# FFT convolution, last tile: four u and v buffers, sums on GpSimd, output jobs moved into the tile before, other transfers and fewer filler products

## The chip, the core and the metric

The kernel runs on one NeuronCore of a Trainium2 chip. The core has five engines that run side by side, each with its own queue in program order: TensorE (PE, matrix products; its weight loads are listed as PEld), VectorE (DVE), ScalarE (ACT), GpSimd (POOL) and SyncE (SP). SP and ACT also issue DMA transfers; sixteen DMA engines carry them. Operands lie in SBUF (128 partitions), products go into PSUM, which has eight banks. Engines wait for each other through semaphores.

The metric is device time in microseconds (us). Before the change it is 263.94 us, the median of three runs (263.47 to 264.06).

## The reference

The reference computes a circular 7 x 7 convolution of an image with 96 channels to 96 channels by a two-dimensional FFT of 224 x 224 points:

```python
H = W = 224; C = 96; K = 7
x: (1, H, W, C) bf16        w: (K, K, C, C) bf16
wp = jnp.pad(w, ((0, H - K), (0, W - K), (0, 0), (0, 0)))
Xf = rfft2(x.astype(float32), axes=(1, 2))
Wf = rfft2(wp.astype(float32), axes=(0, 1))
Yf = einsum('bhwi,hwio->bhwo', Xf, Wf)
y  = irfft2(Yf, s=(H, W), axes=(1, 2)).astype(bfloat16)
```

## The kernel before

The kernel doesn't transform the whole image. Along the height it cuts the 224 rows into eight strips of 28 rows and uses a short transform of each strip (17 frequencies, `NS`; the first and the last are real, `REAL`). Along the width it convolves directly, with taps saved by a fast algorithm that needs sums and differences of neighbouring pixel planes. The width is cut into seven tiles of 32 pixels, tile 0 to tile 6; `TL` is 6, the last. Everything below is about tiles 5 and 6.

Each tile passes through three stages, and the stages of neighbouring tiles run at the same time.

- *Forward transform* (`a_jobs`): products of the input pixels in `xn` with the transform matrix; the results are cast into `xf`. The jobs of tile t + 1 run during tile t, so during tile 6 there are none, and the two `xn` buffers lie idle.
- *Rounds* (`b_round`, line 595), one for each of the 17 frequencies. A round multiplies `xf` and the planes `J` with the transformed weights `WF` into two PSUM banks. The half rounds are counted 0 to 33; after the first bank's products and at the end of the round, `fills` inserts jobs of other stages. ACT scales a part of the first bank into `tt_`; DVE computes u from the first bank and `tt_`, and v from `tt_` and the second bank; the sum of v and u goes into `yf`. The tiles `tt_`, u and v come from `tv_pool` (line 830), two buffers each, so u and v of a round wait for the sum two rounds earlier. The sum (`ysum`, line 671) runs on POOL, or on DVE where `ydve` is set: before, in rounds that also make planes, and in the last tile also in rounds 14, 15 and 16 (line 968). The real rounds 0 and 16 have one DVE sum from a copy by ACT and a bank.
- *Planes* (`jit`, line 563): three DVE operations that make the planes `J` for the next group of three rounds. They are issued in rounds 0, 3, 6, 9 and 12, behind v. A POOL sum of the same round is ordered behind the planes by a semaphore.
- *Put*: after each group of three rounds `yf` is written to a scratch tensor in DRAM, by SP, and in the last tile by ACT in the round that follows, behind that round's scaling (`puts`, line 659). The put after round 16 goes on SP.
- *Output jobs* (`c_jobs`, line 748), eleven for each tile: `load_t` (line 704) reads the scratch tensor back into a tile `tt` with the frequencies in the partitions; a job is two products with the inverse matrix `Gm`, two casts (ACT or DVE, by a planned balance) and, after every second job or so, a DMA to the output. `CQ` (line 43) says how many old and new jobs run during a tile: in tile 5 five of tile 3 and eight of tile 4; in tile 6 three of tile 4 and five of tile 5. `k0` and `k1` are the half rounds between which `pace` spreads them. Only four `tt` tiles and one wide tile `tt2` exist, so a load is issued when an older tile's jobs are done (`pump`, line 802).

The last tile has its own end. Its scratch tensor is split by frequency (`SLAST`): rounds 0 to 8 in `scra` (three puts), then 9 to 11, 12 to 14 and 15 to 16 in three `scrb` (the fourth, fifth and sixth put). The first reloads bring `scra` back in round 11, two transfers. `load_b` (line 723) brings back the three `scrb` parts: the second, third and fourth reload. After round 16 come the six remaining output jobs of tile 5, the first eight products with `GA` on the reloaded `scra` (`first`), filler products on a zero tile `wu` that add nothing to the banks (`WARM`, line 994), and the second products with `GB` (`second`), which need all of `scrb`. Each result is cast into an output tile and written out in eight transfers.

The order on each engine is that in which the program issues the instructions. PSUM banks are handed out in turn, eight in all: two for each round and two for each output job, so a round's bank is the one used four rounds ago, or two rounds ago where every round has a job.

Since helpers record all operations, the profile shows line 99 for nearly all of them; groups are told apart by their tiles: `pb` is a PSUM bank, `yo` or `J` an output tile (the third `J` buffer serves as one).

Of the kernel before, what the change touches and what calls it, by code (L numbers as in the profile page):

```python
# [39 lines left out]
YBUF = 4  # L40
JGB = ((0, 3), (3, 6), (6, 9), (9, 12), (12, 15), (15, 17))
LAG = 4
CQ = {2: (11, 0), 3: (11, 3), 4: (8, 6), 5: (5, 8), 6: (3, 5)}
SH0 = (0, 6, 13, 17)
SH2 = (0, 8, 13, 17)
SH3 = (0, 8, 17)
MERGE = ()
NP2 = 0
WARM = 26
HEAD = ("w",) * 6 + ("x0", "w", "w", "h0", "h1", "w", "w", "x1", "w", "w")  # L50
W1 = 30
ZC = 48
# [12 lines left out]
def kernel(  # L65
# [95 lines left out]
    RB = [sum(KB[:i]) for i in range(NL - 1)]  # L161
    assert sum(KB) == 128
    XW = 2 * TW * C
    xn_bufs = [cpool.tile([R, XW + 32], BF16, name=f"xn{i}") for i in range(2)]

    wtmp_cm = tc.tile_pool(name="wtmp", bufs=1, side="right")
    wtmp = wtmp_cm.__enter__()
# [395 lines left out]
    def jit(t, g):  # L563
# [25 lines left out]
            sub(Jb[:, 5:7, i0:i1], Jb[:, 0:4:2, i0:i1], Jb[:, 1:4:2, i0:i1], ALU.add, 2 * PP * (c1 - c0)),  # L589
        ]  # L590

    yf_cur = {}
    held_x = None

    def b_round(t, s, mid, end, ydve=False, planes=()):
        xf = xf_tiles[t][0:C]
        Jb = jbuf[(t, s)]
        xv = xf.rearrange("c p r s w j -> c p r s (w j)")
        st = {
            0: (Jb[:, 4], xv[:, 0, 1, s], xv[:, 0, 0, s]),  # L600
            1: (Jb[:, 6], Jb[:, 3], Jb[:, 2]),
            2: (Jb[:, 5], Jb[:, 1], Jb[:, 0]),
        }
        for (y0, y1) in (YGRPL if t == TL else YGRP):
            if s == y0:
                yf_cur[t] = (yf_pool.tile([128, YMAX, 2, 2, C], BF16, name="yf"), y0, y1)
        yf, y0, y1 = yf_cur[t]
        yv = yf[:, s - y0]

        def conv(bank, col, m, part, add=False, both=False):  # L610
            pl = st[m][part] if s not in REAL else (xv[:, 0, :, s], Jb[:, 2:4], Jb[:, 0:2])[m][:, part]
            tp = TAPS[m]
            for k, tp_ in enumerate(tp):
                o, wv = bank[:, col:col + C], WF[0:C, slot(s, part), tp_, :]
                if both:
                    o, wv = bank[:, col:col + 2 * C].rearrange("p (m o) -> p m o", m=2), wv.unsqueeze(1).to_broadcast([C, 2, C])
                TE.matmul(o, lhsT=pl[:, (HALO - k) * NJ:(HALO - k) * NJ + 128], rhs=wv,
                          start=(k == 0 and not add), stop=(k == len(tp) - 1 and not both and m != 2 or not add and not both and k == len(tp) - 1))
        b0, b1 = bank(), bank()
        merge = t < 2 and s in MERGE  # L620
        tt_ = tv_pool.tile([128, 4 * C], F32, name="tt_")
        if s in REAL:
            for part in range(2):
                conv(b0, part * C, 0, part)
            held = SE.copy(out=tt_[:, 0:2 * C], in_=b0[:, 0:2 * C])
            if t == s == 0:
                nonlocal held_x
                held_x = held
            mid()
            for mi, m in enumerate((2, 1)):  # L630
                for part in range(2):
                    conv(b1, (mi * 2 + part) * C, m, part)
            VE.tensor_tensor(out=yv.rearrange("p r m o -> p m r o"),
                             in0=tt_[:, 0:2 * C].rearrange("p (r o) -> p r o", o=C).unsqueeze(1).to_broadcast([128, 2, 2, C]),
                             in1=b1[:, 0:4 * C].rearrange("p (m r o) -> p m r o", m=2, r=2), op=ALU.add)
            load["a"] += 110 + 0.9 * 192
            load["v"] += 540
            for f in planes:
                f()
            end()  # L640
        else:
            v = tv_pool.tile([128, 2, 2, C], F32, name="v")
            if merge:
                conv(b0, 2 * C, 0, 0, both=True)
                conv(b0, 2 * C, 2, 0, add=True)
                conv(b0, 3 * C, 1, 0, add=True)
                conv(b0, 0, 0, 1)
                conv(b0, C, 0, 2)
                SE.mul(out=tt_[:], in_=b0[:, 0:4 * C], mul=-0.5)
                u, pr = tt_[:, 2 * C:4 * C].rearrange("p (m o) -> p m o", m=2), tt_[:, 0:2 * C]  # L650
            else:
                for part in range(3):
                    conv(b0, part * C, 0, part)
                conv(b0, 3 * C, 2, 0)
                conv(b0, 4 * C, 1, 0)
                u = tv_pool.tile([128, 2, C], F32, name="u")
                SE.mul(out=tt_[:, 0:3 * C], in_=b0[:, 0:3 * C], mul=-0.5)
                pr = tt_[:, C:3 * C]
            if puts:
                puts.pop(0)()  # L660
            if not merge:
                VE.scalar_tensor_tensor(out=u[:], in0=b0[:, 3 * C:5 * C].rearrange("p (m o) -> p m o", m=2), scalar=-0.5,
                                        in1=tt_[:, 0:C].unsqueeze(1).to_broadcast([128, 2, C]), op0=ALU.mult, op1=ALU.add)
            mid()
            for mi, m in enumerate((2, 1)):
                for pi, part in enumerate((1, 2)):
                    conv(b1, (mi * 2 + pi) * C, m, part)
            VE.scalar_tensor_tensor(out=v.rearrange("p m r o -> p m (r o)"),
                                    in0=pr.unsqueeze(1).to_broadcast([128, 2, 2 * C]), scalar=-2.0,
                                    in1=b1[:, 0:4 * C].rearrange("p (m q) -> p m q", m=2), op0=ALU.mult, op1=ALU.add)  # L670
            def ysum(eng):
                return eng.tensor_tensor(out=yv.rearrange("p r m o -> p m r o"), in0=v[:],
                                         in1=u.unsqueeze(2).to_broadcast([128, 2, 2, C]), op=ALU.add)
            if ydve:
                ysum(VE)
            last = None
            for f in planes:
                last = f()
            if not ydve:
                y = ysum(GE)  # L680
                if len(planes) > 1:
                    tc.add_manual_dep(y.ins, last.ins.name, SYNC, reason="sum after planes")
            load["a"] += 490 if merge else 410
            load["v"] += (560 if ydve else 250 if t < 2 else 0) + (560 if merge else 900)
            end()
        if s == y1 - 1:
            dst, yo0 = scr_tiles[t], 0
            if t == TL:
                i = sum(s >= v for v in SLAST[1:])
                dst, yo0 = scr_tiles[(t, i)], SLAST[i]  # L690

            def put(eng=DE):
                eng.dma_start(out=dst.rearrange("w j s e -> (w j) s e")[:, y0 - yo0:y1 - yo0],
                              in_=yf[:, 0:y1 - y0].rearrange("p s r m o -> p s (r m o)"))
            if t == TL and s < NS - 1:
                puts.append(lambda: put(SE))
            else:
                put()
# [5 lines left out]
    def load_t(t, gi, h):  # L704
        tt = t2_pool.tile([128, 12, 2 * C], BF16, name="tt2") if gi == 2 else t_pool.tile([128, 8, 2 * C], BF16, name="tt")
        tt_tiles[(t, gi, h)] = tt
        sv = scr_tiles[t].rearrange("w j s (r e) -> (j s r) w e", r=2)
        if gi < 2:
            dma(tt[0:112, 0:8], sv[gi * 3 * FR:gi * 3 * FR + 112, h * 8:(h + 1) * 8])
        else:  # L710
            r0 = 6 * FR
            for p0, p1 in ((0, 64), (64, 2 * FR)):
                dma(tt[p0:p1], sv[r0 + p0:r0 + p1, 0:12])
            for j in range(2):
                dma(tt[2 * FR:3 * FR, 4 * j:4 * j + 4], sv[r0 + j * FR:r0 + (j + 1) * FR, 12:16])

    TW2 = 2 * TW * C
    tl_all = xf_bufs[(TL + 1) % 2].rearrange("c p r s w j -> c (p r s w j)")
# [211 lines left out]
    for t in range(2, NT):  # L930
# [9 lines left out]
            add(4 if t == 2 else 0, 26, a_jobs(t + 1))  # L940
        nold, nnew = CQ[t]
        k1 = 2 * NS if t < TL else 2 * NS - 8
        k0 = {2: 15, TL: 6}.get(t, 3)
        km = k0 + -(-(k1 - k0) * nold // (nold + nnew))
        add(k0, km, cj[:nold])
        cn = c_jobs(t - 1)
# [6 lines left out]
        for s in range(NS):  # L953
            now = ()
            if s in plan:
                g = plan[s]
                now = jit(t, g + 1) if g + 1 < len(JGB) else jit(t + 1, 0)
            if s == 2 and t == 2:
                queue_c(0)
            if s == (3 if t in (2, TL) else 2):  # L960
                queue_c(t - 1)
            if t in (3, 4):
                next(gp, None)
            if t == TL and s == SA + 2:
                sv = scr_tiles[(TL, 0)].rearrange("w j s (r e) -> (j s r) w e", r=2)
                for g in range(2):
                    dma(tl_a[g], sv[g * (2 * KA - KAP):g * (2 * KA - KAP) + KAP])
            b_round(t, s, fills(qs, 2 * s), fills(qs, 2 * s + 1), bool(now) or (t == TL and s >= NS - 3), now)
    tail[0] = 1
    load["v"], load["a"] = 1000.0, 0.0  # L970
    while cj:
        cj.pop(0)()
    assert not pend
    for i in range(NL - 1):
        load_b(i)
    for f in outs:
        f()
# [63 lines left out]
```

## Time and profile before

| | us |
|---|---|
| median of three runs | 263.94 |
| the profiled execution's own time | 263.47 |
| its span | 261.7 |
| PE busy | 252.0 |
| DVE busy | 218.4 |
| ACT busy | 196.7 |
| POOL busy | 97.6 |

The profile page lists busy time by engine, the chain of work that ended last, followed back from the last instruction, and groups of instructions. In the timeline each line has the start, the duration, the engine and the operation with its output and inputs; brackets at the end tell how long the engine idled before it and what ended that. SPq and ACTq are the queues of DMA issues of SP and ACT; their durations are those of the issue. The trace also holds the landings of every transfer, one for each DMA engine that took part.

Times are counted from the start of the span. Tile 5's rounds run from about 186 to 216 us, the last tile's from 216 to 243; the end takes from 243 to 261.7. In this execution round 0 of the last tile starts its first products on `xf` at 216.36, round 3 at 220.30, round 6 at 225.60, round 9 at 231.44, round 12 at 236.85 and round 16 at 242.29.

### The profile page before, as it was taken

To read this page: it belongs to the slowest core of one execution; us is meant where nothing else is said; L and a number is where in the kernel's file an instruction comes from. 1 tells how busy PE (TensorE), PEld (TensorE's weight loads), DVE (VectorE), ACT (ScalarE), POOL (GpSimd) and SP (SyncE) were. 2 spreads that over 40 slices of the span, in tenths; PEclk is the share of its full clock that TensorE was granted. 3 is DMA by queue.
4 is the path that set the end of the run, shared out by engine and by line. 5 is a ranking of instruction groups with operands and counts; after the bars stand their busy time and mean duration, and the time that the engine had idled before them with its cause. 6 is when DMAs were issued, how large, how long until landed. Compare 5 with 4: busy or idle time off the path is not lost.

```text
span 261.7 us, 11987 instructions
## 1 busy us (share of the span) xinstructions
PE 252.0 (96%) x5054; PEld 233.2 (89%) x5054; DVE 218.4 (83%) x462; ACT 196.7 (75%) x470; POOL 97.6 (37%) x152
## 2 busy tenths in 40 slices
PE   8999999999999999999999999999999999989983
PEld 2889999999989999989999998999999999979652
DVE  6799998899999889868887788878989799989724
ACT  8889978697745967988988799887988853555423
POOL 7782224464656633232223322334123423423000
PEclk9999999999999999999999999999999999999999
DMA  7995104611111697997967596878849842886996
GB/s 177 272 186 135 48 6 140 177 48 48 48 51 71 183 255 138 302 286 192 271 188 222 143 278 206 212 200 255 275 139 193 288 140 83 206 232 185 236 249 201
DMA packets 47278, 46.88 MB, mean 179 GB/s; under 512 B 35696, under 2 KB 38452, under 8 KB 47224
## 3 DMA queue, kind: packets, MB, share of 16 engines
q1 hardware_dynamic: 46504, 44.64, 62.6%
q10 hardware_dynamic: 720, 1.47, 1.7%
q8 instruction: 39, 0.64, 1.1%
q14 instruction: 15, 0.12, 0.2%
HBM read 24.76 MB, written 21.33 MB: 176 GB/s over the span
## 4 chain that ended last, share of the span: by engine, by line
PE 74%; DVE 10%; DMA 8%; issue 4%; ACT 1%; POOL 1%; SPq 1%; DVEq 0%; ACTq 0%
PE pb L99 68%; PE ps L99 6%; DVE J L99 5%; DMA xn<-in_x_dram 3%; DVE WF L99 2%; DMA tt<-scr 2%; DMA xf<-scrb 2%; DMA scrb<-yf 1%; DVE v L99 1%; POOL yf L99 1%; DVE yf L99 1%; DMA scr<-yf 1%; DVE u L99 1%; SPq L99 1%; ACT xf L99 0%
## 5 line engine op out<-in xcount | busy, mean ns | idle before, releaser
L99 PE MATMUL pb<-WF,J 96*128 96x96 bf16 x2821 | 162.4, 206 | 2.1 <-DVE u L99 0.8
L99 PEld LDWEIGHTS <-J 96*128 96x128 bf16 x2821 | 138.0, 98 | 11.0 <-issue 3.7
L99 POOL TENSOR_TENSOR yf<-v,u 128x384 bf16<-128x384 f32 x79 | 81.4, 1044 | 139.7 <-issue 86.3
L99 ACT CAST xf<-pb 96x408 bf16<-96x408 f32 (+6 forms) x140 | 65.1, 492 | 3.4 <-PE pb L99 1.4
L99 PE MATMUL pb<-WF,xf 96*128 96x96 bf16 x952 | 59.9, 206 | 0.2
L99 DVE TENSOR_TENSOR J<-xf 96x456 bf16<-96x456 bf16 (+3 forms) x85 | 56.0, 698 | 0.0
L99 PEld LDWEIGHTS <-xf 96*128 96x128 bf16 x952 | 47.1, 98 | 1.0 <-PE ps L99 0.6
L99 PE MATMUL pb<-Fm,xn 118*128 118x136 bf16 (+4 forms) x576 | 43.8, 203 | 0.2 <-DMA xn<-in_x_dram 0.2
L99 PE MATMUL pb<-tt,Gm 102*84 102x384 bf16 (+1 forms) x132 | 32.0, 326 | 0.5 <-DVE yf L99 0.4
L99 ACT CAST yo<-pb 84x384 bf16<-84x384 f32 (+1 forms) x61 | 26.2, 482 | 6.2 <-PE pb L99 6.2
L99 PEld LDWEIGHTS <-xn 118*128 118x128 bf16 x576 | 28.6, 97 | 0.5 <-issue 0.4
L99 ACT CAST J<-pb 84x384 bf16<-84x384 f32 (+1 forms) x64 | 27.5, 491 | 0.0
L99 DVE TENSOR_TENSOR J<-J 96x912 bf16<-96x912 bf16 (+2 forms) x42 | 25.4, 604 | 0.0
L99 ACT CAST WF<-pb 96x480 bf16<-96x480 f32 x42 | 21.3, 566 | 0.1
L99 PEld LDWEIGHTS <-wq 128*128 128x128 bf16 (+1 forms) x288 | 19.7, 148 | 0.2
L99 DVE TENSOR_TENSOR yf<-v,u 128x384 bf16<-128x384 f32 x26 | 15.2, 583 | 0.9
L99 PE MATMUL pb<-wq 128*128 128x120 bf16 x192 | 15.3, 224 | 0.0
L99 DVE TENSOR_TENSOR WF<-WF 96x960 bf16<-96x960 bf16 x15 | 14.0, 931 | 1.4 <-ACT WF L99 1.3
L99 PEld LDWEIGHTS <-Gm 102*84 102x84 bf16 (+1 forms) x132 | 11.3, 117 | 1.6 <-issue 0.6
L99 PEld LDWEIGHTS <-wu 128*112 128x112 bf16 (+1 forms) x49 | 6.2, 128 | 6.4 <-issue 3.9
L99 ACT COPY xf<-xf 96x816 bf16<-96x816 bf16 (+4 forms) x18 | 10.8, 659 | 0.0
L99 DVE CAST tt<-pb 112x384 bf16<-112x384 f32 x8 | 4.2, 555 | 6.6 <-PE pb L99 6.2
(397 smaller groups left out, 256.9 us busy)
## 6 DMA issues: line engine op xcount, KB each, us to landing
scr<-yf SPq DMA_DIRECT2D x30, 288.0 KB
xn<-in_x_dram SPq DMA_DIRECT2D x12, 672.0 KB
tt<-scr SPq DMA_DIRECT2D x24, 336.0 KB
out_dram<-yo SPq DMA_DIRECT2D x12, 252.0 KB
out_dram<-J SPq DMA_DIRECT2D x12, 252.0 KB
tt<-scr SPq DMA_DIRECT2D x6, 288.0 KB
wq<-in_w_dram SPq DMA_DIRECT2D x5, 288.0 KB
WF<-in_x_dram SPq DMA_DIRECT2D x2, 672.0 KB
```

Of the source, the lines that this page charges most:

```text
L99: r = fn(*a, **k)
```

## The change

Seven edits, all for tiles 5 and 6 and the end.

- In the last tile u and v no longer come from `tv_pool`: v takes four places in turn in the idle first `xn` buffer, u four in the second (`tv_tile`; the buffers are now allocated with 128 partitions). `tt_` keeps its two.
- In the last tile the sums of rounds 3, 6, 9, 12 and 14 go from DVE to POOL; only round 15 and the real rounds stay on DVE. Those of 3, 6, 9 and 12 are ordered behind the planes of their round.
- In tile 5 eleven jobs of tile 4 run instead of eight; in the last tile none of tile 4 are left, and five of tile 5 run from half round 14, as they did before.
- All four `tt` tiles are thus free when tile 5's reloads are queued in round 3 of the last tile.
- The two reloads of 34 rows for tile 5's wide job become two of 32 and two of 2 rows.
- The second reload (rounds 9 to 11) is issued on SP before round 16, ahead of the last put; it was issued behind it.
- 14 filler products instead of 26.

```diff
-CQ = {2: (11, 0), 3: (11, 3), 4: (8, 6), 5: (5, 8), 6: (3, 5)}
+CQ = {2: (11, 0), 3: (11, 3), 4: (8, 6), 5: (5, 11), 6: (0, 5)}
...
-WARM = 26
+WARM = 14
...
-    xn_bufs = [cpool.tile([R, XW + 32], BF16, name=f"xn{i}") for i in range(2)]
+    xn_all = [cpool.tile([128, XW + 32], BF16, name=f"xn{i}") for i in range(2)]
+    xn_bufs = [xb[0:R] for xb in xn_all]
...
+    xn_f = [xb.bitcast(F32) for xb in xn_all]
+
+    def tv_tile(t, s, name, shape):
+        if t < TL:
+            return tv_pool.tile([128] + shape, F32, name=name)
+        n = 4 * C if name == "v" else 2 * C
+        f = xn_f[name == "u"][:, s % 4 * n:(s % 4 + 1) * n]
+        return f.rearrange("p (a b c) -> p a b c", a=2, b=2) if name == "v" else f.rearrange("p (a b) -> p a b", a=2)
...
-            v = tv_pool.tile([128, 2, 2, C], F32, name="v")
+            v = tv_tile(t, s, "v", [2, 2, C])
...
-                u = tv_pool.tile([128, 2, C], F32, name="u")
+                u = tv_tile(t, s, "u", [2, C])
...
-            for j in range(2):
-                dma(tt[2 * FR:3 * FR, 4 * j:4 * j + 4], sv[r0 + j * FR:r0 + (j + 1) * FR, 12:16])
+            for p0, p1 in ((0, 32), (32, FR)) if t == TL - 1 else ((0, FR),):
+                for j in range(2):
+                    dma(tt[2 * FR + p0:2 * FR + p1, 4 * j:4 * j + 4], sv[r0 + j * FR + p0:r0 + j * FR + p1, 12:16])
...
-        k0 = {2: 15, TL: 6}.get(t, 3)
+        k0 = {2: 15, TL: 14}.get(t, 3)
...
+            if t == TL and s == NS - 1:
+                load_b(0)
...
-            b_round(t, s, fills(qs, 2 * s), fills(qs, 2 * s + 1), bool(now) or (t == TL and s >= NS - 3), now)
+            b_round(t, s, fills(qs, 2 * s), fills(qs, 2 * s + 1), bool(now) if t < TL else s >= NS - 2, now)
...
-    for i in range(NL - 1):
+    for i in range(1, NL - 1):
         load_b(i)
```

## The prediction

> **What bounds the kernel now.** I read the page first, then the waits of TensorE (PE) from tile 5 on, then the timeline of the last tile engine by engine, then the end of the chain of work.
>
> ```profile
> span 261.7 us, 11987 instructions
> ...
> PE 252.0 (96%) x5054; PEld 233.2 (89%) x5054; DVE 218.4 (83%) x462; ACT 196.7 (75%) x470; POOL 97.6 (37%) x152
> ```
>
> PE has work in 96% of the span, so a job moved from one tile to another is not saved. Only idle PE time, and what follows PE's last product, can be won. The waits of PE between 186 and 262 us:
>
> ```profile
> PE pb L99 <- DMA xf<-scrb: 1.2, 1, 1.2
> PE pb L99 <- DVE u L99: 0.8, 1, 0.8
> PE pb L99 <- DVE yf L99: 0.4, 1, 0.4
> ```
>
> Two of the three lie behind the last round. The timeline shows where the 0.8 comes from (rounds 6 to 9 of the last tile), and one line of round 14:
>
> ```profile
> 226.64 1.96 POOL L99 TENSOR_TENSOR yf<-v,u 128x384 bf16<-128x384 f32 x2 [3.21 <-issue]
> 227.67 0.36 DVE L99 SCALAR_TENSOR_TENSOR u<-pb,tt__6883 128x192 f32<-128x192 f32 x1 [0.44 <-POOL yf L99]
> 228.53 0.56 DVE L99 TENSOR_TENSOR yf<-v,u 128x384 bf16<-128x384 f32 x1
> 229.00 1.40 DVE L99 TENSOR_TENSOR J<-xf 96x1824 bf16<-96x1824 bf16 x2
> 230.33 0.62 DVE L99 TENSOR_TENSOR J<-J 96x912 bf16<-96x912 bf16 x1
> 231.27 0.33 PE L99 MATMUL pb<-WF,J 96*128 96x96 bf16 x4 [0.81 <-DVE u L99]
> ...
> 242.33 0.79 DVE L99 TENSOR_TENSOR yf<-v,u 128x384 bf16<-128x384 f32 x1
> ```
>
> Every third round VectorE (DVE) waits for a GpSimd (POOL) sum to free u, does a sum (0.56) and three plane operations (229.00 to 230.95), and PE waits for the bank that round 7's u reads. The end of the chain of work and the queues around it:
>
> ```profile
> 244.38 0.54 DVE yf L99
> 244.92 0.02 issue
> 244.94 3.54 DMA scrb<-yf
> 248.47 0.02 issue
> 248.49 4.40 DMA xf<-scrb
> 252.89 0.14 issue
> 253.03 3.96 PE pb L99 x22
> ```
> ```profile
> 238.54 1.01 SPq L99 DMA_DIRECT2D xf<-scra  x2
> 239.32 0.33 ACTq L99 DMA_DIRECT2D scrb<-yf  x1
> 244.94 0.34 SPq L99 DMA_DIRECT2D scrb<-yf  x1
> 245.32 3.47 SPq L99 DMA_DIRECT2D xf<-scrb  x3
> 247.45 4.39 PE L99 MATMUL pb<-wu 128*112 128x384 bf16 x26
> ```
>
> So the end is set by: last sum (244.92), last put (3.54), its reload (4.40), then 8.7 us of second products, casts and output. The fillers end at 251.84, and PE then still waits 1.19.
>
> **Three jobs into tile 5.** PE: six matmuls, two of a job 0.165 apart; a round with a job takes 1.73, one without 1.40 (starts of rounds 4, 5, 6, 7), so 0.35 a job, 1.0 in all, moved and not saved. Two of the three come before the first products of tile 5's round 12 (nine jobs by then before, eleven after). From there the DVE chain is dense to 222 us, so that chain is 0.70 later at the start of the last tile, PE 1.05. Casts: by the order of the changed program ACT gets four more (0.43) and DVE two (0.54). ACT was busy 13.40 of 15.70 us in 186.3 to 202, DVE 13.46, so they may be hidden or delay banks: from 0 up to 1.0 us (the six nearly unhidden, half on each side). I take 0.2, nearest to the fact that PE waited nowhere in that stretch. The earlier first new job (half round 13, about 197.9) finds its reload landed at 197.5.
>
> **Sums on GpSimd, four buffers.** Gone from DVE: five sums of 0.56 to 0.79 in rounds 3, 6, 9, 12 and 14, and the waits for u (0.44, 0.44, 0.78, 0.43). Late instead: POOL does three sums per group (0.99 each, 1.96 for two), the first ordered behind the planes. And DVE operations with both inputs in SBUF do not run while POOL is in a sum: the 0.79 of round 14 started at 242.33 inside a POOL sum (241.70 to 242.71) and ended 0.41 after it, against 0.56 alone. The planes are of that kind. So a group becomes a loop: planes 1.95, then three sums 2.96, then 0.05 to start, 4.96 (before: 5.17, 5.52, 5.17 from planes to planes). POOL's second sum ended at 223.44, so with the 0.70 the planes start at 224.14, 229.10, 234.06, 239.02; before 223.83, 229.00, 234.52, 239.69. Round 7's u is then 0.1 later than before, and PE's wait, which it ends, stays (about 0.9 instead of 0.81, because PE also comes without three jobs but 1.05 later). After it PE runs through: last product at 243.5 (243.39). End of arithmetic: planes done 240.2, sums 12, 13, 14 to 243.2; ACT holds behind the fourth sum the put (0.33) and the copy of round 16 (0.32), to 243.9; the last sum (0.55) ends at 244.5 instead of 244.92. That is -0.4, with the 0.2 of tile 5 -0.2. Bounds: -0.9 (PE's wait gone too) and +0.8 (1.0 lost in tile 5).
>
> [...]
>
> **Reloads for tile 5's jobs, 32 rows.** The landing records show the two 34-row loads (issued 222.10 and 222.41) arriving on two engines only, last at 228.24; the 64-row load, on sixteen, arrives 3.5 to 4.2 after its issue at 220.84. Now they are four transfers, two issues more on SP (0.27 to 0.67 each). The put before them is 0.70 later (sum of round 15 ends at 219.5), so they are issued from about 221.9 to 225 and land by 227; the first job is due at 227.8. Cost 0; if they come a microsecond late it is 0.5. By the program's semaphores (eight, shared in turn) the next load waits for the 64-row one (about 225), no later than SP is free anyway. All four 112-row loads then go out by about 230.5; before the last two went at 229.28 and 232.74, and 0.5 MB of tile 4's output lay among them, which now goes in tile 5.
>
> **The third put and the first reloads.** The third put is issued at 234.1 as before (its three sums end 0.1 later than the wait that held it). Before, it landed at 238.52, 4.4 later, between a 336 KB load of 232.74 and outputs; a lone put of tile 5 (218.82) landed after 1.7. With only the last outputs beside it I take 2.4: 236.5. The first reloads (238.54) wait for nothing else, so they go 1.8 earlier (bounds 0 and 2.7).
>
> **Second reload ahead of the last put.** It waits for the fourth put, issued at 239.1 (239.32), which before landed at 245.08, behind the first reloads. With these 1.8 earlier: 243.3. The second reload then takes SP until 244.5 (its issue took 1.16), and the last put follows at 244.7 without waiting. The put lands after 1.7 to 3.5: nearest to before, whose fifteen of sixteen arrivals came within 2.4; with the reload beside it 3.0: 247.7. Its reload took 4.40 because the second and third (issued 245.32 and 247.77, landed 250.52 and 252.03) lay ahead; a reload of 336 KB with nothing ahead (193.74) landed after 3.8. With only the third ahead I take 3.6: 251.3, second products at 251.4 instead of 253.03: -1.6 together with the arithmetic. Bounds: put 1.7 and reload 3.0 give -3.4; 3.5 and 4.4 give -0.3; a blocked SP +1.3 (below).
>
> **Fillers.** Twelve fewer at 0.169 are 2.0 us of PE that only covered the reload: 0. They end at 249.6, and PE idles 1.8 instead of 1.19. The granted clock was 1.00 after the 1.19 (252 to 256 us); what a longer idle does no row shows. [...]
>
> **Sum.** -0.2 arithmetic, -1.4 transfers: 261.7 becomes 260.1 of span, the profiled execution's own 263.47 becomes 261.9. That execution is the fastest of the three, 0.47 under the median of 263.94, so I predict 262.3.
>
> **The rivals.** (1) *The last put stuck behind the second reload*, slower: SP is in order, so if the fourth put lands after 243.5 each further microsecond delays the last put; at 245.08 as before, the put goes at 246.3, 1.4 later than 244.94. Less what the shorter queue gives back (0 to 0.9): +0.5 to +1.4, 264.4 to 265.3. For it: that put took 5.8 before. Against: what it stood behind starts earlier. (2) *The queue, not the order, sets the last landing*: reloads two to four land one behind the other (250.52, 252.03, 252.89), and if the same bytes need the same time, only -0.3 to +0.3 remains: 263.6 to 264.2. For it: DMA share above 1.2 in 248 to 252. Against: a share of 0.55 in 246 to 248. (3) *ACT, DVE or POOL full*: the 1.0 of tile 5, or planes locked twice in a group (+1.0), eat the gain: 263.3 to 264.3. (4) *An undisturbed end*, -3.0: 260.9. (5) *A slower clock after a longer idle*: if the reload comes as late as before, PE idles 3.4 instead of 1.19, and no row after tile 1 shows such a gap ahead of products. Were the 24 products of 0.165 to take twice their 4 us for a part or the whole, it would be 264 to 266. [...]
>
> **How the numbers follow.** Forecast (261.5 to 263.2) 0.55, (4) 0.10, (2) 0.13, (1) 0.12, (3) 0.07, (5) 0.03. A measurement here tells 0.2%, 0.53 us. Faster: forecast and (4) and a little of (2) and (3), 0.70; within: 0.15; slower: (1), (5) and the rest, 0.15. The range leaves out the far ends of (4), (1) and (5): 260.7 to 264.6.
>
> **What would show it.** Right: POOL sums in threes of 0.99 with planes starting at their end; PE's wait for u still there near 231; the first reloads at about 236.5; the second reload's issue before 243.5 and the last put within 0.3 of the last sum; last reload landed near 251.3; clock 1.00 to the end. Wrong: first reloads still at 238.5, the last put more than 1 us behind the last sum, new PE waits in tile 5 or on the reload of round 7.

## The result and the profile after

The changed kernel takes 265.79 us in the median of 22 runs (263.78 to 270.0); the kernel before, on the same chip, 263.59 (262.8 to 267.0). The ratio is 1.0062, with a 95% interval of 1.0041 to 1.0082: slower by 0.6%, where 262.3 and faster was forecast. Medians here and below are over all executions, while the ratios leave out those more than 1.5% above their kernel's fastest, so that the two can differ (most in e3 below: median 266.53, without them 265.44). The profiled execution took 265.72 us, span 264.0; that of before 263.47 and 261.7.

The page's head shows nothing of it: TensorE is busy 252.2 us, 252.0 before, and GpSimd 5.5 us more, for the five sums.

```profile
span 264.0 us, 11964 instructions
PE 252.2 (96%) x5042; PEld 232.4 (88%) x5042; DVE 218.1 (83%) x459; ACT 195.9 (74%) x468; POOL 103.1 (39%) x157
```

TensorE's waits between 186 and 264 us answer to the three shown of before. The wait for the last reload has grown from 1.2 to 3.2; the one for round 7's u (0.8) is 0.6 and stands under `xn`, where u now lies (PE goes on at 231.35); the 0.2 for a u belongs to tile 5 (207.91). A wait for a cast by ACT is new.

```profile
PE pb L99 <- DMA xf<-scrb: 3.2, 1, 3.2
PE pb L99 <- DVE xn L99: 0.6, 1, 0.6
PE pb L99 <- ACT yo L99: 0.4, 1, 0.4
PE pb L99 <- DVE yf L99: 0.3, 1, 0.3
PE pb L99 <- DVE u L99: 0.2, 1, 0.2
```

The planes and the GpSimd sums of the last tile, from the timelines of DVE and POOL (`J<-xf` starts a group's planes; 1.40 is what its two operations take undisturbed):

```profile
223.64 1.98 DVE L99 TENSOR_TENSOR J<-xf 96x1824 bf16<-96x1824 bf16 x2
228.27 2.22 DVE L99 TENSOR_TENSOR J<-xf 96x1824 bf16<-96x1824 bf16 x2
233.97 1.40 DVE L99 TENSOR_TENSOR J<-xf 96x1824 bf16<-96x1824 bf16 x2
```
```profile
222.39 1.96 POOL L99 TENSOR_TENSOR yf<-xn,xn 128x384 bf16<-128x384 f32 x2 [2.68 <-issue]
226.29 2.92 POOL L99 TENSOR_TENSOR yf<-xn,xn 128x384 bf16<-128x384 f32 x3 [1.95 <-issue]
231.16 2.92 POOL L99 TENSOR_TENSOR yf<-xn,xn 128x384 bf16<-128x384 f32 x3 [1.95 <-issue]
```

The first two groups, begun inside sums that end at 224.35 and 229.21, take 1.98 and 2.22: they are held until the POOL sum is over, as forecast. Up to here the arithmetic is about where the prediction had it, in part by luck: this execution was 0.45 us ahead of that of before when its first put went out (26.49, before 26.94). The break comes in ACT's queue, in the same stretch of the timeline:

```profile
229.25 0.33 ACTq L99 DMA_DIRECT2D scra<-yf  x1
235.46 0.33 ACTq L99 DMA_DIRECT2D scra<-yf  x1
235.83 0.85 ACT L99 CAST yo<-pb 56x384 bf16<-56x384 f32 x2 [3.01 <-DMA scra<-yf]
240.06 0.33 ACTq L99 DMA_DIRECT2D scrb<-yf  x1
244.16 0.33 ACTq L99 DMA_DIRECT2D scrb<-yf  x1
```

ACT stands for 3.01 us until a transfer `scra<-yf` has landed, and issues the third put only then, at 235.46. The trace gives the semaphore of each transfer: its 227 transfers use eight in turn, each 28 or 29 times, and none of the 219 with a predecessor on its semaphore went out before that one's last landing. Second and third put have the same semaphore: the second, issued at 229.25, landed at 235.39, and the third waited on ACT for that. Not all of the 3.01 is due to that: the GpSimd sums that the third put brings out ended at 234.08 (231.16 and 2.92), so the semaphore held the put for 1.4 us. Behind the waiting put on ACT stood scalings and casts, so u, v and the sums came late from round 9 on. The end of the chain of work, and SP's queue:

```profile
246.35 0.40 DVE J L99
246.76 4.26 DMA scrb<-yf
251.02 0.02 issue
251.04 2.62 DMA xf<-scrb
253.65 0.14 issue
253.79 5.62 PE pb L99 x22
```
```profile
221.77 7.60 SPq L99 DMA_DIRECT2D tt<-scr  x10
238.58 1.04 SPq L99 DMA_DIRECT2D xf<-scra  x2
246.36 0.30 SPq L99 DMA_DIRECT2D xf<-scrb  x1
246.76 0.48 SPq L99 DMA_DIRECT2D scrb<-yf  x1
248.46 2.88 SPq L99 DMA_DIRECT2D xf<-scrb  x2
```

The fourth put landed at 246.35, the second reload waited for that, and the last put stood behind it in SP's queue: it went out 1.26 after the last sum (245.50), as soon as the reload's issue was over (the cast that the chain names there, 246.35, only ended at the same time). The second products start 0.76 later than before. Then they take 5.62 instead of 3.96, and the windows of the end (columns: window, its length, busy time with counts of PE, PEld, DVE, ACT and POOL, granted clock, DMA share, GB/s) show why:

```profile
252.00:254.00 2.00, 0.21 (x2) 0.21 (x3) 0.00 (x0) 0.00 (x0) 0.00 (x0) 1.00 0.89 272
254.00:256.00 2.00, 2.00 (x10) 1.30 (x9) 1.46 (x3) 1.24 (x3) 0.00 (x0) 0.72 0.91 300
256.00:258.00 2.00, 2.00 (x8) 1.38 (x7) 0.68 (x2) 0.96 (x2) 0.00 (x0) 0.50 0.83 267
258.00:260.00 2.00, 1.72 (x10) 1.05 (x8) 1.62 (x4) 1.21 (x3) 0.00 (x0) 0.93 0.44 134
```

After an idle of 3.24 us the granted clock is 0.50 from 254.86 to 258.27, for 3.41 us. 0.76 and 1.66 are 2.42, less 0.12 that the outputs behind are shorter: the 2.3 of the span.

### The profile page after: what moved, and what is told of

Its sections match the earlier page's. It is cut to its first block, busy times and chain, and to the rows that moved or that the text cites. A ratio compares the mean times of both kernels' runs of the same rounds, so it can differ in the third digit from the quotient of the medians.

```text
span 264.0 us, 11964 instructions
## 1 busy us (share of the span) xinstructions
PE 252.2 (96%) x5042; PEld 232.4 (88%) x5042; DVE 218.1 (83%) x459; ACT 195.9 (74%) x468; POOL 103.1 (39%) x157
## 4 chain that ended last, share of the span: by engine, by line
PE 71%; DVE 12%; DMA 6%; ACT 4%; issue 3%; POOL 1%; DVEq 0%; ACTq 0%
PE pb L99 65%; PE ps L99 6%; DVE J L99 5%; DVE WF L99 2%; DMA scra<-yf 2%; ACT xf L99 2%; DVE xn L99 2%; DMA scrb<-yf 2%; DMA xf<-scrb 1%; POOL yf L99 1%; ACT WF L99 1%; DMA scr<-yf 1%; DVE v L99 1%; DVE u L99 1%; DVE yf L99 1%
## 5 line engine op out<-in xcount | busy, mean ns | idle before, releaser
L99 POOL TENSOR_TENSOR yf<-v,u 128x384 bf16<-128x384 f32 x70 | 72.5, 1049 | 124.9 <-issue 71.9
L99 DVE TENSOR_TENSOR J<-xf 96x456 bf16<-96x456 bf16 (+3 forms) x85 | 57.4, 715 | 0.0
L99 POOL TENSOR_TENSOR yf<-xn,xn 128x384 bf16<-128x384 f32 x14 | 13.7, 1000 | 10.7 <-issue 9.7
L99 DVE TENSOR_TENSOR yf<-v,u 128x384 bf16<-128x384 f32 x20 | 11.6, 579 | 0.7
## 6 DMA issues: line engine op xcount, KB each, us to landing
out_dram<-yo SPq DMA_DIRECT2D x12, 252.0 KB
out_dram<-J SPq DMA_DIRECT2D x12, 252.0 KB
```

Source lines behind the costliest of these rows:

```text
L99: r = fn(*a, **k)
```

## The experiments

Theories: (A) the third put's wait for the second put's landing makes all that follows late; (B) the GpSimd sums are too slow; (C) the fillers alone, through the clock; (F) the moved jobs cost more than they give back; (H) the 32-row loads do it. Further letters are explained where they are used. Each time is a median, with its distance from that of the kernel before on the same chip in the same hour; in brackets stands the ratio with its 95% interval.

**Fillers, reload, semaphore and sums, each undone in the changed kernel.**

```diff
-WARM = 14
+WARM = 26
```


> The changed kernel with 26 filler products instead of 14, nothing else. Theories of the loss: (A) the third put waits for the second put's semaphore, so ACT stands still for 3.0 us, all reloads come late, the last put goes behind the second reload, and PE then idles 3.24 us and runs its last products at half clock; (B) the sums on GpSimd hold up the planes and so the whole last tile; (C) the fillers alone: without the twelve the clock falls, and the rest is neutral. Here all three let the fillers end near 252.5, PE idle about 1.2, and the granted clock stay 1.00 to the end, which takes 1.6 us from the 5.62 of the second products. By C the time equals the kernel before (263.6). By A and B 0.7 to 0.9 us remain, since the second products still start at 253.8 instead of 253.0: 264.3 to 264.5.

264.87, 1.60 above before (1.0055, 1.0033 to 1.0078). By theory C it should have equalled the kernel before.

```diff
-            if t == TL and s == NS - 1:
-                load_b(0)
...
-    for i in range(1, NL - 1):
+    for i in range(NL - 1):
         load_b(i)
```


> The changed kernel with the second reload behind the last put again. By A the last put goes at about 245.5, with the last sum, 1.26 earlier than 246.76; the second reload is issued at 246.4 as now, so the last reload has it and the third ahead again and takes 4.4 instead of 2.62: second products at about 253.0 to 253.9, between 0 and 0.8 earlier, and the idle time and the half clock stay (2.4 to 3.3 us): -0.2 to -1.0 against the changed kernel, more where the clock holds. If the order on SP is the main loss, it is -1.3 and with the clock -2.9. By B and C nothing.

264.77, 1.50 above (1.0039, 1.0013 to 1.0065).

```diff
             if t == TL and s == NS - 1:
                 load_b(0)
+            if t == TL and s == 8:
+                SE.dma_start(out=GA[0:2 * SA, 0, 0:B], in_=G[0:2 * SA, 0:B])
```


> The changed kernel with one more small transfer on ACT's queue in round 8 (18 rows of the inverse matrix to the place where they already stand), which moves the third put on to another of the eight semaphores, one whose transfer landed long before. By A the third put goes right behind its sums, at about 234.1 instead of 235.46; ACT and PE are not held (round 12 starts 0.7 earlier); the first reloads start at 236.5 to 237.5 instead of 238.58; the second reload is issued before the last sum, the last put within 0.3 of it; second products at 251.5 to 252.5, idle below 3 us, clock 1.00: 262 to 263. By B the time stays at 265 to 266, since the planes come as now. By C the clock still falls, with 2 fewer us of fillers: the time is 264.5 or more.

The added transfer writes again what `GA` already holds; it takes a turn of the semaphores, and 1.33 us of ACT's queue. 266.53, 3.26 above (1.0066, 1.0029 to 1.0103), although the profiled execution is a good one (263.27). In it the third put went at 233.87, the fourth landed at 243.54, the last put went within 0.05 of its sum and the second products started at 252.02. But the wait has only moved: now a reload `tt<-scr` of SP has the second put's semaphore. SP's waits from 220 to 243:

```profile
SPq L99 <- DMA scra<-yf: 7.6, 2, 5.9
```

Reloads and outputs then pile up with the third put and the first reloads. And a second thing shows: the second products ended 1.0 earlier than before, the span only 0.1. The last eight stores took 2.9 to 3.7 from issue to landing instead of 2.1 to 2.4, behind the four output stores that SP had held back. The end is limited by transfers as well as by the chain.

```diff
-            b_round(t, s, fills(qs, 2 * s), fills(qs, 2 * s + 1), bool(now) if t < TL else s >= NS - 2, now)
+            b_round(t, s, fills(qs, 2 * s), fills(qs, 2 * s + 1), bool(now) or (t == TL and s >= NS - 3), now)
```


> The changed kernel with the sums of rounds 3, 6, 9, 12 and 14 of the last tile on DVE again, the four buffers kept. The third put still shares the second one's semaphore. By A the third put is still held to about 235, since the second put still goes out among four reloads: -0.5 to +0.3, the clock still falls. By B planes start when v is done, nothing waits for GpSimd: round 9 about 0.5 earlier, the end 1 us earlier and the clock holds: 263 to 264.

267.09 in six runs, 3.82 above (1.0107, 1.0061 to 1.0153). Theory B falls: with the sums back on DVE it is slower still. Fillers and reload each take part of the loss; neither is all of it.

**Two undone together, jobs undone, fillers alone.**

The dummy transfer of e3 with `WARM = 26`:

> The third put on its own semaphore together with 26 fillers (e3_own_semaphore with the fillers of before). e3 had a profile of 261.6 us span with the second products at 252.02, but most of its other executions lay at 265 to 269 us. Theory A (the shared semaphore made the put late; the remaining loss of e3 is the clock, which falls when TensorE idles too long behind 14 fillers, and with 26 the idle is 2.0 shorter): third put at 233.9, second products near 252.0 at granted clock 1.00, and nearly all executions at 263.0 to 264.0, median 263.4. Theory D (the executions of e3 are long because the transfers themselves come later there): the median stays above 265.5 with the clock at 1.00 in the second products. Theory E (the last stores are bound by the bytes of the four held stores, so no start of the second products before 253 can shorten the span): span 261.3 to 261.9, not 260.6 even where the second products start at 252.0.

265.87, 2.20 above (1.0076, 1.0045 to 1.0108): theory A in this form failed, D came nearer. TensorE's timeline of that profile:

```profile
248.45 1.53 PE L99 MATMUL pb<-xf,GA 80*112 80x384 bf16 x4 [1.12 <-DMA xf<-scra]
249.77 5.42 PE L99 MATMUL pb<-wu 128*112 128x384 bf16 x26
255.03 0.98 PE L99 MATMUL pb<-xf,GB 128*112 128x384 bf16 x5
```

The first reload's second half came 8.56 after its issue, the granted clock was 0.50 from 248.46 to 251.87, the 26 fillers took 5.4 and ran past the last reload's landing (253.55): here the fillers themselves held the second products for 1.3.

`WARM = 26` and the second reload behind the last put, so that four buffers, sums, jobs and 32-row loads are left:

> The changed kernel with 26 fillers and with the second reload behind the last put, as before: four buffers, the sums on GpSimd, the five jobs and the 32-row loads are left. Theory A: the third put still waits for the second one's landing (issued near 235.5), the last put goes out right behind the last sum (245.9), second products near 253.0, TensorE idle under 0.5, clock 1.00, and 263.4 to 264.0 (before: 263.3). Theory F (the five late jobs and the GpSimd sums cost by themselves): 264.5 or more, like e1 and e2.

264.33, 0.66 above (1.0012, 0.9980 to 1.0044): between the two, and no longer to be told from before.

```diff
-CQ = {2: (11, 0), 3: (11, 3), 4: (8, 6), 5: (5, 11), 6: (0, 5)}
+CQ = {2: (11, 0), 3: (11, 3), 4: (8, 6), 5: (5, 8), 6: (3, 5)}
...
-        k0 = {2: 15, TL: 14}.get(t, 3)
+        k0 = {2: 15, TL: 6}.get(t, 3)
```


> The changed kernel with eight old and three new jobs as before, from half round 6: three jobs fewer in tile 5 and three more in the last tile; by the order of transfers the third put then shares its semaphore with an older transfer than the second put. Theory A: third put issued within 0.5 of its sum (near 234), last put not held more than 0.3 behind its sum; second products before 252.8; what clock is left depends on the idle behind 14 fillers, so 263.3 to 265.5. Theory F (three more jobs in tile 5 are the cost): 0.7 less than the changed kernel, with the third put still waiting for the second one's landing and the last put behind the second reload.

264.60, 0.93 above (1.0036, 1.0006 to 1.0067). The third put went out on time (234.62), yet the second products started at 255.12 in the profile, for SP stood until the second put had landed (235.23), and TensorE waited 2.9 for the first reloads.

The kernel before with `WARM = 14` and nothing else:

> The kernel before with 14 fillers in place of 26, nothing else. TensorE's idle before the second products grows from 1.19 to 3.2 or 3.3 (12 x 0.17 us less). Theory C (an idle of that length costs the clock): granted clock 0.5 in much of the second products in most executions, these 1.5 to 1.7 us longer, median 264.5 to 265.2. If the idle does not matter: 263.3, clock 1.00.

265.50, 1.83 above (1.0047, 1.0007 to 1.0086). Twelve fillers fewer cost time by themselves, between 0.2 and 2.3 us by the interval. That is not theory C as it stood, since the fillers alone don't explain the change: put back in it (e1), they took the loss from 2.20 to 1.60 only. Its profiled execution is one of the shorter ones (264.48) and did not lose the clock, though TensorE idled nearly as long as in the changed kernel:

```profile
PE pb L99 <- DMA xf<-scrb: 3.1, 1, 3.1
```
```profile
248.89:252.30 3.41, 1.68 (x11) 1.06 (x9) 0.00 (x0) 0.00 (x0) 0.00 (x0) 1.00 1.08 180
252.30:255.71 3.41, 2.08 (x12) 1.58 (x13) 1.58 (x3) 1.48 (x4) 0.00 (x0) 1.00 0.81 296
```

The windows, 3.41 us long like the falls of the clock in the other executions, are counted back from this execution's own fall, at 262.53, when TensorE was done; each of the two holds about half of the idle, and the clock column stays at 1.00. Ten of the twelve runs have a mean clock of 0.983 to 0.994, the other two (263.11 and 264.48 us) 1.000; the kernel before has 0.997 in the median. That the clock makes e8 slower is read from these means; its one profile doesn't show it.

**Single edits added to the kernel before.** Buffers and sums (`tv_tile`, the wider `xn` and the `ydve` argument of the diff):

> The kernel before with two of the seven edits: four buffers for u and v in the last tile, and the sums of its rounds 3, 6, 9, 12 and 14 on GpSimd. Measured from the issue of the first put (26.93 in the profile before), the last sum ended 218.0 us later in the kernel before (218.7 in the run with 14 fillers) and 216.8 later in e7_jobs_back. Theory G (the sums and buffers are worth about 1.2 of arithmetic when no put is held): last sum 216.6 to 217.2 after the first put, TensorE waits for u near 231 gone or under 0.5. Theory E (the transfers of the end eat it: the reloads land no earlier): second products within 0.4 of before in the same count, median 263.3 to 264.0; if the gain reaches the end: 262.3 to 262.9.

262.48, 1.18 below before (0.9976, 0.9952 to 1.0001), as theory G has it with the gain reaching the end, and, run again as base of e16:

> The same kernel as e9_buffers_sums (four buffers and the sums on GpSimd added to the kernel before), as base for e16 on the same chip: median 262.2 to 262.9, 0.9 to 1.4 below before.

262.35, 1.59 below (0.9945, 0.9914 to 0.9975). This version beats both kernels. In e9's profile TensorE has a single wait left between 186 and 262, and the chain ends 1.2 earlier than before:

```profile
PE pb L99 <- DMA xf<-scrb: 1.5, 1, 1.5
```
```profile
242.81 0.57 DVE yf L99
243.40 3.64 DMA scrb<-yf
247.05 4.65 DMA xf<-scrb
251.70 0.14 issue
251.84 3.96 PE pb L99 x22
```

On top of it the 32-row loads:

```diff
-            for j in range(2):
-                dma(tt[2 * FR:3 * FR, 4 * j:4 * j + 4], sv[r0 + j * FR:r0 + (j + 1) * FR, 12:16])
+            for p0, p1 in ((0, 32), (32, FR)) if t == TL - 1 else ((0, FR),):
+                for j in range(2):
+                    dma(tt[2 * FR + p0:2 * FR + p1, 4 * j:4 * j + 4], sv[r0 + j * FR + p0:r0 + j * FR + p1, 12:16])
```


> e9_buffers_sums with the reloads of 34 rows split into 32 and 2 rows, nothing else: the next load then waits less (the 34-row loads land 5.8 after their issue before, the 32-row ones 3.6 to 4.2 in the changed kernel), so four wide loads are queued closer together and the second put lands later (6.1 instead of 3.6). If the crowd costs: the third put or a load waits for the second put's landing, first reloads later than in e9 by 0.5 to 1.5, median 0.3 to 1.0 above e9. If the split is neutral: within 0.3 of e9.

266.37, 2.71 above before (1.0088, 1.0063 to 1.0114), 3.9 more than e9 and far more than expected. SP's waits from 220 to 243, first of e9, then of e10:

```profile
SPq L99 <- DMA scra<-yf: 6.9, 3, 2.7
```
```profile
SPq L99 <- DMA scra<-yf: 8.2, 2, 6.0
```

In both a transfer of SP shares the second put's semaphore. In e9 that put lands 3.86 after its issue; in e10, where two wide reloads were queued 1.7 and 1.3 ahead of it and an output 0.7, it takes 5.81. SP stands for 6.0, and tile 4's outputs and the last wide reloads go out together at 234.7 to 238.9, right ahead of the first reloads (239.23 and 241.11 instead of 237.27 and 237.64). The queue is not all of the 3.9. TensorE then waited 1.6 and 0.8 for these reloads, the granted clock was 0.50 from 248.99 to 252.40, and the fillers ran on at half speed:

```profile
249.30 5.92 PE L99 MATMUL pb<-wu 128*112 128x384 bf16 x26
```

The last reload had landed at 253.32; the fillers held the second products until 255.06. Counted from each execution's first put, the landing is 1.1 later than in e9 and the second products are 2.7 later.

The reorder alone, on the kernel before:

> The kernel before with the second reload issued ahead of the last put, nothing else. Before, the fourth put landed at 245.1 and the last sum ended at 244.9, so the last put is held by 0.5; it then moves beside the second reload (4.3 instead of 3.5 in the changed kernel), and its own reload is shorter (2.6 instead of 4.4). That adds up to -0.5 to 0: second products 252.5 to 253.0 and a median of 263.0 to 263.7. If the blocked queue is what costs (rival 1 of the prediction): the last put over 1 behind its sum in this kernel too, median 264.2 or more.

264.06, 0.40 above (1.0029, 1.0000 to 1.0058): put and reload as expected (4.30, 2.70), the put held 0.9 behind its sum, second products at 252.80 instead of 253.03, but the held stores start 1.5 later and the span is 0.3 longer. Hold and median lie between the two expectations.

The jobs alone (the diff of e7, reversed, on the kernel before):

> The kernel before with the job counts of the change (eleven in tile 5, none of tile 4 and five of tile 5 from half round 14 in the last tile), nothing else. In the eight profiles with eleven jobs in tile 5 the put after its round 11 goes out 189.7 to 190.1 after the first put, in the three with eight jobs 188.4 to 189.1. Theory F (the three jobs cost in tile 5 and the last tile gives back less): this put at 189.7 or later, last sum 0.3 to 1.0 later than before in the same count, median 264.0 to 264.8. If they are only moved: last sum within 0.3 of before, 263.3 to 263.8.

264.85, 1.19 above (1.0045, 1.0021 to 1.0070). The put named there is the one after tile 5's round 14, not 11; it went out at 189.73 from the first put, and the last sum was 1.2 later than before.

**The 32-row loads from three sides.** The changed kernel with 34-row loads; the kernel before with 32-row ones; e6 with 34-row ones:

> The changed kernel with the 34-row reloads of before; the other six edits stay. Theory H (the split lets SP queue three or four wide reloads at once, the second put then lands 6 instead of 4 after its issue, and what shares its semaphore waits): second put lands within 4.5 of its issue, third put within 0.5 of its sum, second products 1.5 to 2.5 earlier than in the changed kernel in the count from the first put (227.3 there), median 263.0 to 264.3. Theory I (the single costs add, the split costs only beside outputs of tile 4): within 0.5 of the changed kernel's 265.8.

> The kernel before with the 34-row reloads split into 32 and 2 rows, nothing else. Theory H: SP stands at a reload or output until the second put has landed (about 235 instead of 232.3), tile 4's outputs and the last wide reloads go out 2 to 3 later, the first reloads at 239.2 or later with the second of them 1.5 to 2.5 later than before, TensorE waits over 1.0 for them before the first products, and the median is 2 to 4 above before: 265.6 to 267.6. If the split cost only with the faster sums of e10: within 0.5 of before.

> Buffers, GpSimd sums and the job counts of the change, with 34-row reloads, 26 fillers and the second reload behind the last put; e6_fillers_reload is the same with 32 rows (264.33, 0.66 above before in its call). If the costs add (jobs +1.2 on e9): within 0.3 of before, 263.4 to 264.0. If the split costs here too (theory H): 0.7 or more below e6's distance to before. If it costs nothing in this company: 0.4 to 0.9 above before, like e6.

e13: 264.78, 0.94 above (1.0044, 1.0011 to 1.0076), between the two expectations; the third put went out on time (234.85, 1.0 earlier than in the changed kernel in the count from the first put), and what it has beside e15 is reorder and fillers (TensorE idles 2.5). But its second put still took 5.33, not under 4.5: with all `tt` tiles free it is slow without the split too, so that part of theory H is wrong. e14: 264.42, 0.58 above (1.0008, 0.9971 to 1.0046), not to be told from before; its profile is of an execution 3.5 longer than its median and is not read. e15: 263.41, 0.43 below (0.9991, 0.9961 to 1.0020). e15 and e6 differ in nothing but the split, and show theory A at its cleanest. ACT's queue, second and third put, first in e15, then in e6:

```profile
229.66 0.33 ACTq L99 DMA_DIRECT2D scra<-yf  x1
234.52 0.33 ACTq L99 DMA_DIRECT2D scra<-yf  x1
```
```profile
229.85 0.33 ACTq L99 DMA_DIRECT2D scra<-yf  x1
235.84 0.33 ACTq L99 DMA_DIRECT2D scra<-yf  x1
```

In both the second put takes 5.9 to 6.0 (four wide reloads go out just ahead of it, since all `tt` tiles are free). With 34 rows the third put has the first put's semaphore and goes when its sum is done; with 32 rows two more transfers have shifted the turn, and it stands for the second put, 1.4 later counted from the first put. The last sum is then about 1.0 later, and the median goes from 0.43 below before to 0.66 above. That the put is held is plain in the traces; the difference in time is within the two intervals.

**The reorder where the last put should be free:** `load_b(0)` ahead of the last put, added to e9.

> e9_buffers_sums with the second reload ahead of the last put. In e9 the fourth put landed at 242.6 and the last sum ended at 243.4, so the second reload goes out at 242.7 and the last put is not held (within 0.3 of its sum). Premise of the prediction (the reorder pays where the put is not held): put 4.3 and last reload 2.7 as in the kernel before with this edit, 7.0 instead of 8.3: second products 0.8 to 1.3 earlier than in e17 in the count from the first put, median 0.3 to 1.0 below e17 if the last stores follow. If the reorder loses by itself (the put beside the reload takes longer than the queue gives back, or the four held stores, issued later, hold the last stores): the same as e17 or up to 0.6 more.

262.39 (0.9955, 0.9921 to 0.9988), against 262.35 of the same kernel without it. In the profile the fourth put landed 1.57 later than in e17 (at 244.18, e17's at 242.61), so the last put was held 0.6 all the same, and the last stores took 2.7 to 3.1 instead of 2.1 to 2.4. The reorder gains nothing.

**The path from before to the change,** by adding the edits one after the other; each number is the distance of a median to before on its chip:

| edits | kernel | us | ratio |
|---|---|---|---|
| buffers, GpSimd sums | e9, e17 | -1.18, -1.59 | 0.9976, 0.9945 |
| and the jobs | e15 | -0.43 | 0.9991 |
| and the 32-row loads | e6 | +0.66 | 1.0012 |
| and the second reload ahead | e1 | +1.60 | 1.0055 |
| and 14 fillers | the change | +2.20 | 1.0062 |

A single step of this ladder (0.6 to 1.2) is about as large as the uncertainty of one distance. What intervals alone establish: buffers with sums are faster (e17, and e16 with the reorder; e9's interval just reaches 1), the jobs alone and the fillers alone are slower, and the split on top of e9 is slower. The costs do not add: on its own the split can't be told from nothing, with tile 4's outputs in the last tile and the faster sums it is 3.9, the clock's part in it.

## Why the prediction was wrong, point by point

The second products were forecast at 251.4 and started at 253.79. Of these 2.4 us the last sum has 0.8 (245.50; 244.7 forecast), the last put behind the second reload 1.26 (0), put and last reload 0.3 (6.88; 6.6). The half clock then added 1.66. Two of the prediction's signs of being right came, the GpSimd sums in threes and the wait for u near 231. So did two of its signs of being wrong, the first reloads still at 238.5 and the last put more than 1 us behind the last sum; of the third, a new wait of TensorE in tile 5, there are 0.2 us.

Counted from each execution's first put, since executions differ by up to 2 us before it:

| | tile 5's fifth put | third put | last sum ends | second products |
|---|---|---|---|---|
| before | 188.4 | 207.2 | 218.0 | 226.1 |
| after | 189.8 | 209.0 | 219.0 | 227.3 |
| e9 | 188.4 | 206.2 | 216.7 | 225.2 |
| e15 | 189.8 | 207.6 | 218.1 | 225.5 |
| e6 | 190.1 | 209.0 | 219.1 | 227.1 |

- *Three jobs into tile 5, 0.70 later:* mis-sized. It is 1.4 (189.8 against 188.4; ten profiles with eleven jobs 189.7 to 190.1, eight with eight jobs 188.4 to 189.1, e14's left out). The prediction had set aside 0 to 1.0 more for the casts and taken 0.2; whether the casts are the rest is open. As it assumed, nothing comes back: from e9 to e15 the last sum, too, is 1.4 later. In both, the groups of three GpSimd sums start 4.86 and 4.89 apart: the last tile's rounds go by the loop of planes and sums, and three jobs fewer there save nothing.
- *Sums on GpSimd, -0.4 with the 0.70 of the jobs in it, TensorE's wait for u stays:* right in mechanism and about right in size. Three sums take 2.92 (2.96 forecast), planes begun in a sum end behind it (1.98 and 2.22), the groups follow each other after 4.87 (4.96), and the wait near 231 is there (0.61; 0.9). In the trace of before, too, all 32 DVE operations with both inputs in SBUF that start in a POOL sum end behind it, by 0.17 to 0.97 us, while 66 of the 84 u and v that start in one, with a PSUM bank among their inputs, end in it. Without the jobs the forecast comes to -1.1; alone, the edit brings the last sum 1.25 forward (1.15 in e17), and TensorE's wait for u goes. It is the one part that pays.
- *32-row loads, cost 0:* the failed step that began the loss. The 32-row loads landed by 227.03, those of 2 rows by 227.67, as forecast in time for the first job. But the prediction applied the turn of the eight semaphores to the next load only, and did not follow it further: two more transfers, with the jobs moved, put the third put onto the second put's semaphore, whose landing at 235.39 it then waited for. With 34 rows (e13) or with the jobs back (e7) it went out on time.
- *Third put at 234.1, landed 236.5, first reloads 1.8 earlier:* issued at 235.46, landed at 238.56 (3.1; 2.4 forecast), first reloads at 238.58 (before 238.54). The prediction left the second put as it was (3.61 from issue to landing in the trace of before); with four wide reloads just ahead of it, which its own text had moved there, it took 6.14. (The lone put of 218.82, said to land after 1.7, has its first of sixteen arrivals then and its last at 1.87; it served as a bound only.)
- *Second reload ahead of the last put:* rival 1 happened, given 0.12. The fourth put landed at 246.35 instead of 243.3, the last put was held by 1.26. Put and last reload together were forecast well (6.6; 6.88), but the price was the hold, and e16 shows no gain where the hold is down to 0.6.
- *Fillers 0, idle 1.8, clock 1.00:* idle 3.24, granted clock 0.50 for 3.41 us, 1.66 longer: rival 5, given 0.03. This is not so in every execution: seven of the 22 have a mean clock of 0.999 or 1.000 and a median of 264.51, the others 0.982 to 0.994 and 266.19. Nor was the step free where the idle came near the 1.8: e2, with an idle of 2.0 in its profile, has a mean clock under 0.995 in seven of its twelve runs (the kernel before in two of 29 beside it), and e8, with 3.06, lost 1.83. That the longer idle costs 0 was the author's estimate, and no run shows it: the runs showed the 1.66 here and the 1.83 of e8. Nor does a row of before show the products at twice their time that rival 5 counts with; the changed kernel shows a clock of 0.50 for 3.41 us of them.
- *The 8.7 us behind the second products' start, constant:* not so where the chain gets shorter. In e3 and e16 the held stores are then still moving, and the last stores take 2.7 to 3.7 instead of 2.1 to 2.4.

The rivals were priced one by one. What happened was 1 and then 5, and 5 because of 1: each made the next one's condition true.

## What to carry to other kernels

Where transfers share a few semaphores in turn, as the 227 here share eight, a transfer added or split also moves every later one to another of them (from e15 to e6 the third put went from the first put's to the second put's, and out 1.4 later), so list which earlier transfer each urgent one must wait for, and ask how long that one takes in the new order. Filler products that cover a wait need not be free to drop: twelve fewer cost the kernel before 1.83 in the median (e8), and in the changed kernel, with its second products 0.76 later, the granted clock then was 0.50 for 3.41 us; price their removal with the wait at its longest, not as forecast. And when several edits come as one, try them alone: here two of the edits together were worth 1.2 to 1.6 us in the medians, and the other four hid it.

## What the runs showed of the hardware

Where the granted clock fell before TensorE's last products, it was 0.50 for 3.41 us each time (254.86 to 258.27 in the changed kernel, 248.46 to 251.87 in e5, 250.55 to 253.96 in e7), and where a second fall came at the end of the same execution, it came a whole number of 3.41 us after the first (two in the changed kernel, at 261.69; four in e5, at 262.1). The clock fell after an idle of 3.24, one of 2.40 (e4) and two of 1.56 and 0.82 (e10), and did not after one of 3.06 (e8) and one of 2.50 (e13). So the length of the gap alone does not decide it. Nor does TensorE's modelled busy time in the 3.41 us before: after 1.45 us of it the clock fell in e4 (253.24 to 256.65), after 1.39 it stayed at 1.00 in e13 (249.04 to 252.45). What decides it, and why executions of e2, e8 and the changed kernel differ so much among themselves, no run shows.

A transfer's wait for a shared semaphore was taken on the issuing engine, with all that was queued behind it: it held the third put on ACT for 1.4 us here, and in e10 it kept SP for 6.0 us in one piece, where SP's three such waits in e9 came to 6.9 and none was over 2.7. In this program, where 227 transfers share eight semaphores in turn, these runs show what that costs in time.
